# Reordering the last blocks of a single-core attention-and-MLP kernel, with a tail by priority, a held filler and one layernorm tile on ScalarE

## The chip, the cores and the metric

The kernel runs on one core of one Trainium2 chip. The metric is the device time of one execution in microseconds (us); a kernel's time is the median of several executions. A ratio between two kernels is the mean time of one kernel's runs over that of the other's of the same rounds on the same chip, so it is not quite the ratio of the medians quoted here. A clock given with a run is the mean granted TensorE clock.

The engines are written as the profile has them: PE is TensorE (PEld its weight loads), ACT is ScalarE, DVE is VectorE, POOL is GpSimd, SP is SyncE.

## The reference, cut to what matters

The input x is 2048 tokens by 448, in bfloat16. Attention has 16 heads of 28.

```python
xn = layernorm(x)
q, k, v = split(xn @ wqkv)                            # 16 heads of 28
s  = softmax(q @ k.T * 28 ** -0.5) @ v @ wo           # attention
g  = silu(gelu(xn @ w1 + b1) @ w2 + b2)               # dense layers, 448 -> 1792 -> 448
out = x + s * g
```

## The kernel before

Attention is done in blocks. A block is one head group (4 heads) on one query chunk (512 queries); there are 4 x 4 = 16 blocks of 64 score tiles, each 128 keys by 512 queries, 1024 tiles in all. A small scheduler in Python runs when the kernel is built. It holds every piece of work as a task with an engine, a planned duration and a priority, simulates the five engines, and writes each engine's instructions in the order that comes out. A change of a threshold or a priority therefore moves instructions about, nothing else.

```python
NP = 21                       # buffers of 128x512 for exp'd scores (P)
THS    = (8.0, 4.0, 7.0, 8.0, 4.0, 7.0, 9.0, 6.0, 6.0, 8.0, 8.0, 8.0, 8.0, 8.0, 7.0, 3.0)   # one per block
SLACKS = (6.0, 5.0, 3.0, 5.0, 2.0, 6.5, 9.0, 6.5, 3.0, 4.0, 7.0, 6.0, 8.0, 6.0, 8.0, 3.0)
HAM_WIN, HAM_LOW, DUM = 3.4, 0.85, 0.17
...
g, c = b // C, b % C          # block b: head group g on query chunk c
```

**Scores and exps.** TensorE writes three score tiles into PSUM (`ring`), ScalarE takes the exponential of the three in one instruction (a unit), and TensorE multiplies them with the values into `acc`. ScalarE is the bound, so the last tile of some units goes to VectorE instead, which scales it (0.69 us) and works out the exponential as a polynomial in integer and float arithmetic (`p_exp2`, five more instructions):

```python
def pick_late(self, u):       # does VectorE take the last tile of unit u?
    ...
    left = (n - 1 - r) / 3.0 * 1.364 + SLACKS[m // 64]       # time to the end of the block, plus a slack
    ...
    bl = K.backlog()                                          # what VectorE has queued
    if not K.ys or bl > THS[m // 64] or bl + 4.8 > left or sub > LATE_SUB:
        return False

def p_exps(self):
    ...
    yield ("until", lambda: all(K.PPREV[m] is None or K.pv_done[K.PPREV[m]] for m in ms))   # P buffer free?
    yield _Task(ACT, fexp, ...)

def p_pv(self):               # value matmuls; the last ones of a block wait for all of its VectorE tiles
    ...
    yield ("until", lambda: K.exp_m >= ms[-1] and K.E_done >= first - 1 and (
        not end or len([x for x in K.late_ready if K.sub_of(x[0]) == b]) == K.late_left[b]))
    ...
    if end:
        K.spawn(K.p_epi(b) if b < NBLK - 1 else K.p_epi4(first - NBLK + 1), 0.5)
```

**The end of a block** normalizes it. GpSimd splits the reciprocals of the row sums in two bfloat16 parts, and TensorE spreads these over the partitions:

```python
def p_epi(self, b):
    yield _Task(DVE, ...tensor_copy(E, K.acc)...)                                  # eviction
    yield _Task(PE, ...)                                                           # row sums
    yield _Task(DVE, ...reciprocal(K.rc, bank[:, 0:16])..., 0.26, 0.0, 1)
    yield _Task(POOL, ...tensor_copy(K.rhi, K.rc)..., 0.2, 0.0, 1)
    yield _Task(POOL, ...tensor_tensor(K.rlo, K.rc, K.rhi, ALU.subtract)..., 0.22, 0.0, 1)
    yield _Task(PE, ...)                                                           # spread rhi, rlo
    yield _Task(DVE, ...tensor_tensor(dst, bank2, E, ALU.mult)..., 0.7, 0.0, 1)
```

**Output.** When a chunk's four head groups are done, each of its four output tiles takes an output matmul, a multiplication by the gate g (0.62 us) and an addition of x (0.39 us) on VectorE, and a store. The last block is cut in three parts, so that only the last output tile is left at the very end (`p_epi4`, `p_norm4`, `p_last`):

```python
def p_norm4(self, t):
    yield _Task(PE, ...matmul(bank[:, 0:128], K.selb, E)..., 0.1, 0.12, 3)
    yield _Task(DVE, ...reciprocal(R, bank[:, 0:128])..., 0.96, 0.0, 1)
    yield _Task(DVE, ...tensor_tensor(dst, E, R, ALU.mult)..., 0.3, 0.0, 1)

def p_last(self, t):
    yield K.t_wo(ps, tok, c, t, (0, 1, 2), 3)
    yield ("until", lambda: K.on4[t])
    yield K.t_wo(ps, tok, c, t, (3,), 3)
    yield from K.t_oev(ps, tok, c, t)
```

**Filler.** A task of priority 95 adds empty matmuls when the planned TensorE activity of the last 3.4 us falls below 85%, to keep the granted clock up (`p_busy`, `pe_low`).

**Start.** x of chunk 0 is loaded in halves over two queues; VectorE does the layernorm statistics of all its tiles; x of chunk 1 is loaded after the first weights on SyncE's queue.

## Time and profile before

| | kernel before |
|---|---|
| time, median of 3 | 483.63 us (483.53 to 483.73) |
| the profiled execution by itself | 484.9 us, span 483.1 us, mean clock 0.993 |
| first exp begins | 13.14 us |
| first exp's start to last exp's end | 463.32 us |
| last exp's end to the end of VectorE | 4.46 us |
| VectorE's end to the end of the span (last store) | 2.15 us |
| tiles that VectorE takes | 76 of 1024 |

The four rows from the first exp to the last store are read from the trace and add up to the span. They are the frame.

How many tiles VectorE takes is read from the groups of instructions, as the count of the instruction that evicts a score tile to VectorE (line, engine, operation, tiles, count; busy us, mean ns; idle before it and its releaser):

```profile
L1183 DVE TENSOR_SCALAR x_sb<-ring 128x512 int32<-128x512 f32 x68 | 46.8, 688 | 14.2 <-PE ring L1129 13.0
L1274 DVE TENSOR_SCALAR x_sb<-misc 128x512 int32<-128x512 f32 x8 | 5.5, 686 | 1.8 <-PE misc L1270 1.8
```

That is 68 + 8 = 76 tiles; ScalarE has the other 948.

### The profile page before, as it was taken

The numbers are of one execution on the slowest core, as the hardware profiler recorded it, in microseconds if no ns is written. First come the engines' busy times: TensorE is split into PE (matmuls) and PEld (weight loads), VectorE is DVE, ScalarE is ACT, GpSimd is POOL, SyncE is SP. The second block draws the span as 40 slices with busy tenths as digits, with TensorE's granted clock in tenths as the row PEclk, the third lists the DMA queues.
The fourth block names the chain that finished last, engine by engine and source line by source line (L and its number), as shares of the span: only waits on it lengthen the run. The fifth ranks groups of instructions, "written<-read, shape, count | busy, mean of one in ns | idle before, by whom it ended". The sixth has DMA issues, their size and how long they took to land.

```text
span 483.1 us, 10155 instructions
## 1 busy us (share of the span) xinstructions
PE 438.5 (91%) x4232; PEld 168.1 (35%) x4268; DVE 407.6 (84%) x592; ACT 468.8 (97%) x390; POOL 43.2 (9%) x77
## 2 busy tenths in 40 slices
PE   6999899998889898999989988999999999999995
PEld 5442333332223333332323343333333333333453
DVE  8946888989978989989878749899997999889785
ACT  5999999999999999999999999999999999999994
POOL 7470000000010000000101000010100100100001
PEclk9998999999999999999999999999999999999998
DMA  8501000000000000000400000000101010011011
GB/s 247 149 9 28 1 0 2 1 2 2 0 1 1 1 1 1 1 2 1 134 1 0 1 2 0 1 2 1 38 1 40 1 38 1 23 37 58 3 39 39
DMA packets 8288, 11.08 MB, mean 23 GB/s; under 512 B 1650, under 2 KB 6898, under 8 KB 8243
## 3 DMA queue, kind: packets, MB, share of 16 engines
q1 hardware_dynamic: 8098, 10.21, 7.0%
q8 instruction: 33, 0.54, 0.5%
q10 hardware_dynamic: 144, 0.23, 0.1%
q14 instruction: 13, 0.10, 0.1%
HBM read 8.61 MB, written 1.84 MB: 22 GB/s over the span
## 4 chain that ended last, share of the span: by engine, by line
ACT 45%; PE 32%; issue 17%; DVE 5%; ACTq 0%; DVEq 0%
ACT P L1160 42%; PE ring L1129 9%; PE acc L1346 6%; PE misc L1065 4%; PE acc L857 3%; PE misc L695 2%; ACT h L1044 2%; PE misc L1007 1%; PE acc L839 1%; PE misc L949 1%; PE misc L1442 1%; PE ring L1007 1%; ACT w L1080 1%; PE ring L949 1%; DVE kT L1298 0%
## 5 line engine op out<-in xcount | busy, mean ns | idle before, releaser
L1160 ACT ACTIVATE P<-ring 128x1536 bf16<-128x1536 f32 (+1 forms) x350 | 428.9, 1469 | 1.7 <-PE ring L1129 1.5
L1129 PE MATMUL ring<-qT,kT 32*128 32x512 bf16 (+2 forms) x1144 | 136.5, 360 | 26.1 <-ACT P L1160 22.0
L1346 PE MATMUL acc<-P,vaug 128*32 128x512 bf16 (+2 forms) x1074 | 95.0, 363 | 1.0 <-issue 0.5
L1129 PEld LDWEIGHTS ring<-qT,kT 32*128 32x128 bf16 x1144 | 35.5, 91 | 132.8 <-ACT P L1160 123.5
L1183 DVE TENSOR_SCALAR x_sb<-ring 128x512 int32<-128x512 f32 x68 | 46.8, 688 | 14.2 <-PE ring L1129 13.0
L1065 PE MATMUL misc<-w,h 128*128 128x448 bf16 x224 | 52.3, 355 | 0.1
L1415 POOL CAST rhi<-rc 128x16 bf16<-128x16 f32 x15 | 10.3, 686 | 402.5 <-DVE rc L1413 255.6
L857 PE MATMUL acc<-ident,zero 128*128 128x128 bf16 x516 | 44.8, 221 | 0.0
L1346 PEld LDWEIGHTS acc<-P,vaug 128*32 128x32 bf16 x1074 | 24.4, 93 | 51.0 <-issue 46.6
L857 PEld LDWEIGHTS acc<-ident,zero 128*128 128x128 bf16 x516 | 29.8, 98 | 21.3 <-issue 19.4
L1007 PE MATMUL misc<-xnT,w 128*128 128x512 bf16 x127 | 35.9, 382 | 1.3 <-issue 0.8
L990 DVE CAST h<-misc 128x512 bf16<-128x512 f32 x35 | 24.1, 688 | 8.1 <-PE misc L1007 7.0
L1304 DVE SCALAR_TENSOR_TENSOR x_sb<-x_sb,kT 128x1024 uint16<-128x1024 int32 (+1 forms) x24 | 26.7, 1111 | 0.5
L1302 DVE SCALAR_TENSOR_TENSOR kT<-kT 128x1024 f32<-128x1024 f32 (+1 forms) x24 | 26.6, 1110 | 0.5
L1298 DVE SCALAR_TENSOR_TENSOR kT<-kT 128x1024 f32<-128x1024 f32 (+1 forms) x24 | 26.5, 1104 | 0.6
L1300 DVE SCALAR_TENSOR_TENSOR kT<-kT 128x1024 f32<-128x1024 f32 (+1 forms) x24 | 26.4, 1102 | 0.2
L1065 PEld LDWEIGHTS misc<-w,h 128*128 128x128 bf16 x224 | 17.3, 97 | 23.9 <-issue 12.1
L1007 PE MATMUL ring<-xnT,w 128*128 128x512 bf16 x82 | 19.3, 380 | 2.0 <-ACT h L1044 1.6
L1298 DVE SCALAR_TENSOR_TENSOR w<-w 128x1024 f32<-128x1024 f32 (+1 forms) x18 | 20.3, 1128 | 0.3
L1304 DVE SCALAR_TENSOR_TENSOR x_sb<-x_sb,w 128x1024 uint16<-128x1024 int32 (+1 forms) x18 | 20.3, 1130 | 0.2
L1300 DVE SCALAR_TENSOR_TENSOR w<-w 128x1024 f32<-128x1024 f32 (+1 forms) x18 | 20.3, 1130 | 0.2
L1302 DVE SCALAR_TENSOR_TENSOR w<-w 128x1024 f32<-128x1024 f32 (+1 forms) x18 | 20.3, 1129 | 0.1
(154 smaller groups left out, 449.6 us busy)
## 6 DMA issues: line engine op xcount, KB each, us to landing
h<-in_A_x_dram SPq DMA_DIRECT2D x4, 448.0 KB, 3.3
w<-in_B_w_dram SPq DMA_DIRECT2D x1, 1568.0 KB, 7.3
x_sb<-in_A_x_dram SPq DMA_DIRECT2D x3, 448.0 KB, 5.2
w<-in_B_w_dram SPq DMA_DIRECT2D x1, 1344.0 KB, 9.4
out_dram<-h SPq DMA_DIRECT2D x6, 224.0 KB, 1.9
h<-in_A_wqkv_dram SPq DMA_DIRECT2D x3, 168.0 KB, 5.5
out_dram<-h SPq DMA_DIRECT2D x4, 112.0 KB, 1.7
wo<-in_A_wo_dram SPq DMA_DIRECT2D x16, 24.5 KB
```

Of the source, the lines that this page charges most:

```text
L857: ins = eng.matmul(K.acc[:, 0:128], K.zero[:, :], K.ident[:, :], start=False, stop=True, skip_group_check=True)
L990: yield _Task(DVE, lambda eng: eng.tensor_copy(dst, bank), [tok], wr, 0.69, 0.0, 2)
L1007: ins = eng.matmul(bank, K.w1[:, kt, ft * 128:(ft + 1) * 128], K.xnT[:, kt, c * 512:(c + 1) * 512], start=(kt == 0), stop=(kt == KT - 1))
L1065: ins = eng.matmul(ps, hv[:, ft, t * 128:(t + 1) * 128], K.w2[:, ft, :], start=(ft == 0), stop=(ft == FT - 1))
L1129: return eng.matmul(K.ring[:, RB[m], col:col + nq], K.kT[32 * j:32 * j + 32, g, t * 128:(t + 1) * 128], K.qT[32 * j:32 * j + 32, g, c * 51 ...
L1160: return eng.activation(K.P[:, p0:p0 + n, :], K.ring[:, b0:b0 + n, :], ACTF.Exp, scale=SM_SCALE)
L1183: yield _Task(DVE, lambda eng, m=m, i=i, half=half: eng.tensor_scalar(K.ysb[i][:, 512 * half:512 * half + 512], K.ring[:, RB[m], :], SM_SC ...
L1298: yield _Task(DVE, lambda eng: eng.scalar_tensor_tensor(u, v, EXP_A, v, op0=ALU.add, op1=ALU.mult), [tv], [tu], d1, 0.0, 4)
L1300: yield _Task(DVE, lambda eng: eng.scalar_tensor_tensor(u, u, EXP_B, u, op0=ALU.add, op1=ALU.mult), [tu], [tu], d1, 0.0, 4)
L1302: yield _Task(DVE, lambda eng: eng.scalar_tensor_tensor(u, v, EXP_D, u, op0=ALU.mult, op1=ALU.add), [tv, tu], [tu], d1, 0.0, 4)
L1304: yield _Task(DVE, lambda eng: eng.scalar_tensor_tensor(pl.bitcast(dt.uint16), y, 2.0 ** -9, u, op0=ALU.mult, op1=ALU.add), ty + [tu], [K. ...
L1346: return eng.matmul(K.acc[32 * j:32 * j + 32, q0:q0 + nq], K.vaug[:, t, 4 * g + j, :], ap[:, col:col + nq], tile_position=(0, 32 * j), sta ...
```

## The change

Its intent: let both last blocks work on the last query chunk, so that the outputs of the other three chunks are out of the way of the last block; order the tail by priority, looking ahead for a more important task that is about to be ready; hold the filler matmuls back while the end of a block is on its way; move one small addition from GpSimd to VectorE; and shorten the start with ScalarE's sums and an earlier load of x. The thresholds of the offload were tuned again with it. The cuts leave out, among others, two planned durations in the last gate (the tanh 0.87 us for 0.47, the multiplication 1.03 for 0.85).

```diff
+GC = [(b // C, b % C) for b in range(11)] + [(3, 0), (3, 1), (3, 2), (2, 3), (3, 3)]
-THS = (8.0, 4.0, 7.0, 8.0, 4.0, 7.0, 9.0, 6.0, 6.0, 8.0, 8.0, 8.0, 8.0, 8.0, 7.0, 3.0)
-SLACKS = (6.0, 5.0, 3.0, 5.0, 2.0, 6.5, 9.0, 6.5, 3.0, 4.0, 7.0, 6.0, 8.0, 6.0, 8.0, 3.0)
+THS = (8.0, 4.0, 9.0, 8.0, 4.0, 7.0, 9.0, 6.0, 6.0, 8.0, 8.0, 4.0, 8.0, 4.0, 7.0, 5.0)
+SLACKS = (6.0, 8.0, 3.0, 5.0, 2.0, 6.5, 9.0, 6.5, 3.0, 4.0, 7.0, 6.0, 8.0, 6.0, 3.0, 3.0)
+TAIL = 18
 ... # the scheduler
-            self.pe_hist.append((start, start + t.dur))
+            self.pe_hist.append((start, start + t.dur * t.w))        # w: 0.15 and 0.3 for two thin matmul groups
-                    if s is not None:
+                    if s is not None and not (self.hold and p[3].E == PE and p[3].prio >= 90):
+            if self.exp_m >= MTOT - TAIL and E in (PE, DVE):
+                for s2, p2 in sorted(((c[0], c[1]) for c in cand), key=lambda c: c[0]):
+                    if p2[3].E == E and p2[3].prio < p[3].prio and s2 < s + p[3].dur - 0.1:
+                        s, p = s2, p2
+                        break
 ... # the start: loads, and one layernorm tile of chunk 0 on ScalarE
+        K.dma(ACT, lambda eng: eng.dma_start(K.x_sb[:, 1, :, :], xr[1]), K.s_x[1], writes=[K.b_x[1]], land=6.5)
-        ld(K.x_sb[:, 1, :, :], xr[1], K.s_x[1], [K.b_x[1]], 8.0)
+    def p_sums(self, i):
+        yield _Task(ACT, lambda eng: eng.activation(junk, x, ACTF.Copy, accum_out=K.st6[:, i, 0:1]), ...)
+        yield _Task(DVE, lambda eng: eng.tensor_scalar(m, K.st6[:, i, 0:1], 1.0 / D, None, op0=ALU.mult), ...)
+        yield _Task(ACT, lambda eng: eng.activation(junk, x, ACTF.Square, bias=m, scale=-1.0, accum_out=K.st6[:, i, 1:2]), ...)
 ... # the end of the last gate
-            yield _Task(POOL, lambda eng: eng.tensor_tensor(o, o, fb[:, 3, :], ALU.add), ..., 0.85, 0.05, 0)
+            yield _Task(DVE, lambda eng: eng.tensor_tensor(o, o, fb[:, 3, :], ALU.add), ..., 0.4, 0.0, 0)
 ... # the block order, in the scores, the value matmuls and the outputs
-                    g, c = b // C, b % C
+                    g, c = GC[b]
 ... # the end of a block: filler held from the last value matmuls to the eviction
             if end:
+                K.hold = True
 ...
         K.E_done = b
+        K.hold = False
 ... # the tail: priorities 0 to 2 for the last tile; the output matmuls split by head group
-        yield K.t_wo(ps, tok, c, t, (0, 1, 2), 3)
+        for g in range(G - 1):
+            yield K.t_wo(ps, tok, c, t, (g,), 3)
-        yield K.t_wo(ps, tok, c, t, (3,), 3)
+        yield K.t_wo(ps, tok, c, t, (3,), 3 if t < 3 else 1)
```

## The prediction

> **What bounds the kernel now.** I read the page's busy shares first, then ScalarE's groups and its waits, then a table of stretches, and last the timelines of the two ends, where ScalarE isn't the whole story.
>
> The busy line and the costliest group of the page (line, engine, operation, tiles, count; busy us, mean ns; idle before it):
>
> ```profile
> PE 438.5 (91%) x4232; PEld 168.1 (35%) x4268; DVE 407.6 (84%) x592; ACT 468.8 (97%) x390; POOL 43.2 (9%) x77
> ...
> L1160 ACT ACTIVATE P<-ring 128x1536 bf16<-128x1536 f32 (+1 forms) x350 | 428.9, 1469 | 1.7 <-PE ring L1129 1.5
> ```
>
> ScalarE (ACT) is busy 97% of the span, nearly all in L1160, the exps of the attention scores, and it sat idle only 1.7 us before them. The table of stretches (length; then busy us of PE, PEld, DVE, ACT, POOL; granted TensorE clock, DMA share, GB/s) cuts the run at the first exp (13.14 us) and at the end of ScalarE's exp work (476.05 us):
>
> ```profile
> 13.14:476.05 462.91, 426.92 (x4140) 160.65 (x4174) 391.78 (x545) 461.15 (x373) 31.63 (x47) 1.00 0.05 16
> 44.00:46.00 2.00, 2.00 (x10) 0.35 (x9) 0.87 (x2) 1.85 (x2) 0.00 (x0) 0.50 0.00 0
> 46.00:48.00 2.00, 1.84 (x16) 0.68 (x13) 1.41 (x3) 1.16 (x1) 0.00 (x0) 0.85 0.00 0
> 476.05:483.10 7.05, 2.34 (x25) 0.92 (x25) 4.28 (x9) 0.87 (x2) 2.06 (x2) 0.79 0.15 49
> ```
>
> So the time is three terms: a start of 13.1 us, a middle of 462.9 us in which ScalarE is idle only 462.91 - 461.15 = 1.76 us, and a tail of 7.05 us. Most of the idle 1.76 us is one hole: at 44 to 46 us the granted clock falls to 0.50, and ScalarE is then short of scores. The timeline shows the hole (start us, us, engine, line, tiles, [idle before <- releaser]):
>
> ```profile
> 44.75 1.03 PE L695 MATMUL misc<-xnT,wq 128*128 128x512 bf16 x2
> ...
> 46.84 3.71 ACT L1160 ACTIVATE P<-ring 128x1536 bf16<-128x1536 f32 x3 [0.96 <-PE ring L1129]
> ```
>
> Two projection matmuls took 1.03 us where, at full clock, such a pair at 35.80 took 0.60; the scores queued behind them came late, and ScalarE stood for 0.96 us. The tail's timeline:
>
> ```profile
> 475.57 0.89 ACT L1160 ACTIVATE P<-ring 128x512 bf16<-128x512 f32 x1
> ...
> 476.70 0.41 PE L1346 MATMUL acc<-P,vaug 128*32 128x128 bf16 x16
> ...
> 477.16 0.29 DVE L1377 CAST E_sb<-acc 128x128 bf16<-128x128 f32 x1 [0.27 <-PE acc L1346]
> 477.44 0.63 DVE L1451 TENSOR_TENSOR h<-ring,h 128x448 bf16<-128x448 f32 x1
> ...
> 477.81 0.22 PE L1388 MATMUL ring<-E_sb,selb 128*128 128x128 bf16 x1
> 478.06 0.96 DVE L1391 RECIPROCAL w<-ring 128x128 f32<-128x128 f32 x1
> 478.11 1.03 POOL L1097 TENSOR_TENSOR h<-h,w 128x448 bf16<-128x448 bf16 x1
> ...
> 479.88 0.62 DVE L1451 TENSOR_TENSOR h<-ring,h 128x448 bf16<-128x448 f32 x1 [0.16 <-PE ring L1442]
> 480.54 0.39 DVE L1453 TENSOR_TENSOR h<-h 128x448 bf16<-128x448 bf16 x1
> ```
>
> This is a chain: last exp, value matmul (PV), eviction, row-sum broadcast, reciprocal, multiply, output matmul, gate, residual, store. The last VectorE (DVE) instruction ends at 480.93, so the store takes the last 2.2 us.
>
> **What the Trainium skill says.** "Perfetto Trace Analysis", section Identifying the Most-Contended Engine, takes occupancy as a fair measure of distance to the limit on ScalarE: the 97% agrees. "TensorE: Matmul & The Clock Gate", section What's actually happening, says the clock falls to half when a monitor finds TensorE idle over windows of about 3.4 us. The trace has the half clock (0.50), though the record there counts PE busy for all of the 2.00 us. "ScalarE: Activation LUTs", section What ACT_TABLE_LOAD costs, gives 186 ns + 0.833 ns per element for an ACTIVATE with immediate operands and 93 ns more for a pointer operand: for 448 elements 0.56 us, and 0.65 us with a bias pointer. The trace agrees: the 448-element copy at L714 takes 0.56 us. "GPSIMD Engine Reference", section 3.1, has a two-input add about twice as slow on GpSimd as on VectorE; here the 448-element pair is 1.03 against 0.39 us.
>
> **The change part by part.**
>
> *The start.* One of the first chunk's four layernorm tiles leaves VectorE: a statistics instruction of 0.61 us goes; a ScalarE Copy (est. 0.56 us, sum) and Square (est. 0.65 us, squares) come, with two tiny VectorE scalings (0.07 to 0.14 each, as colK's 0.14). ScalarE idles from 2.0 to 5.3 us, so room exists. But the chain is serial: Copy, scale, Square, scale, Ln. Both x halves are there by about 3.9 us; VectorE does two statistics to 4.95, an aggregate to 5.2, the third to 5.8; the mean's scaling is about as early as that third (a tie), so I put it at 5.85, Square 5.95 to 6.65, scaling, Ln at about 6.85 against 6.75 before. So the second half gains nothing directly. The gain is that the first half's two normalizations (0.37 each) run about 0.6 us earlier, off the second half's way (all four sat in 6.63 to 8.53). The second load of x, issued now from ScalarE's queue at about 1.2 rather than 3.40 (its landing took 5.2 us, to 8.6), lets chunk 1's statistics run earlier; before, those at 9.54 held back a critical copy that began at 10.13. Against it, 448 KB now share the DMA engines with the weights that ScalarE relays at 5.73. Net: 0.3 us earlier, anywhere from 0.3 later to 0.9 earlier.
>
> *The hole.* The scheduler's account of TensorE activity now counts the 12 one-column matmuls at 40.74 (0.44 us in all) at 0.15 of their planned time, and the epilogues' four-column ones at 0.3, so it adds filler where the clock fell. At 38 to 42 us these are just what the account overrated. I give it a 65% chance to fill the 0.96 us: 0.6 us.
>
> *Exps moved from ScalarE to VectorE.* A unit of three tiles follows the last by 1.33 us (chain of waits: 121.64, 122.97; 134.22 and 136.88 for two), one of two tiles by 14.88 / 16 = 0.93 us. So a tile taken away saves 0.40 us of ScalarE. On VectorE it costs 0.69 + 0.4 + 4 x 0.69 = 3.85 us alone, or about 3.3 in a pair (0.69 + (0.68 + 4 x 1.13) / 2). Now 68 + 8 = 76 tiles go there. The block order puts chunk 2's last head group at block 14 and the three others one block earlier. So the four output tiles of chunk 2, at 0.62 + 0.39 = 1.01 us, leave the last block (8 gates and only 2 moved exps there now): 4.0 us of VectorE come free where its idle time was 0.6 us, enough for one more tile, perhaps two; the threshold for that block goes from 3 to 5. But block 12 takes chunk 0's output work with 1.3 us idle, thresholds of blocks 11 and 13 go from 8 to 4, and VectorE's total work is the same. Filler held back at block ends frees part of the 4.1 us in which evictions waited for filler. Net: 1 to 2 tiles more, 1.5 x 0.40 = 0.6 us.
>
> *The tail.* PV waits for the last exp (ends 476.46) and then behind output matmuls until 476.70; split by head group and ordered by priority, it can go at about 476.55: 0.15 us. The broadcast matmul at 477.81 stood behind four output matmuls, one slot of 0.19 us. In all 0.35 us, if VectorE's other gate (477.44 to 478.07) also stays out of the reciprocal's way. The gate's add (1.03 us on GpSimd, ends 479.14) wasn't what ended the wait: the last gate started at 479.88 behind TensorE. Moved to VectorE (0.39 us) it should fit while TensorE does its last matmul; it gains nothing and could cost up to 0.3.
>
> **Sum:** 0.3 + 0.6 + 0.6 + 0.35 = 1.85 us, so 483.63 - 1.85 = 481.8; I say 481.7.
>
> **The rivals.** (1) *ScalarE stays the bound and little moves:* no tile more is offloaded, the hole moves elsewhere. For it: VectorE's total work is equal and it is 84% busy already; then only the ends count, 0.65 us, giving 483.0. (2) *TensorE's clock becomes the limit:* held filler and lighter accounting shift the activity, and half-clock stretches of a microsecond each open new holes. For it: one did so before; against: only one in 463 us, and held filler pauses below 1 us. It would be 484. (3) *The x load in front delays the weights,* ScalarE waits in order, and the first exp comes 0.5 later: 482.6 or so. (4) *Everything takes:* three tiles (1.2), hole (1.0), start 0.8, tail 0.6: 480.0.
>
> **Range and chances.** The four terms are about independent, each uncertain by 0.3 to 0.6 us, so about 1 us together; I take 480.1 to 483.2. A 2% change is 9.7 us, more than start, hole, tile and tail savings together could give; the added work is less still. Same 0.98.
>
> **What would show it.** First exp at about 12.8 us (start right) or past 13.1 (wrong). No clock below 0.9 and no ScalarE wait near 0.9 us before 50 us (hole). 77 or 78 scores evicted by VectorE at what are now L1183 and L1274, three or four of them in the last block (offload). From the last exp's end to the last VectorE instruction 4.1 us rather than 480.93 - 476.46 = 4.47, and the broadcast matmul directly behind its eviction (tail). The number is wrong if the middle gains a new wait of ScalarE for scores, or if the tile count moves by more than three.

## The result, and the profile after

The changed kernel took 484.13 us (median of 6, 484.01 to 484.83) against 483.68 us for the kernel before beside it (median of 6, 483.53 to 483.75). The ratio is 1.0013, with a 95% interval of 1.0 to 1.0026: the same within 2%, as expected, but on the slower side, and above the predicted range of 480.1 to 483.2 us.

The page's busy line and the exps' group of the changed kernel, and its two groups of tiles that go to VectorE:

```profile
PE 438.1 (91%) x4242; PEld 168.7 (35%) x4278; DVE 395.5 (82%) x570; ACT 471.4 (98%) x394; POOL 40.1 (8%) x76
...
L1191 ACT ACTIVATE P<-ring 128x1536 bf16<-128x1536 f32 (+1 forms) x350 | 429.8, 1496 | 0.7 <-PE ring L1160 0.5
...
L1214 DVE TENSOR_SCALAR x_sb<-ring 128x512 int32<-128x512 f32 x65 | 44.7, 688 | 16.0 <-PE ring L1160 15.1
L1305 DVE TENSOR_SCALAR x_sb<-misc 128x512 int32<-128x512 f32 x8 | 5.5, 685 | 1.8 <-PE misc L1301 1.8
```

VectorE's busy time fell from 407.6 to 395.5 us, and it takes 65 + 8 = 73 tiles, three fewer than before. ScalarE's idle time before the exps fell from 1.7 to 0.7 us, yet its work grew. The table of stretches of the changed kernel (columns as in the prediction; as there, the middle is cut a little before the last exp's end, which is at 476.45 us here and at 476.46 before, so that it is 0.4 to 0.6 us shorter than in the frame above):

```profile
13.12:475.85 462.73, 426.91 (x4155) 161.19 (x4188) 380.82 (x523) 461.97 (x373) 29.54 (x47) 1.00 0.05 16
44.00:46.00 2.00, 1.46 (x14) 0.41 (x12) 1.76 (x3) 2.00 (x3) 0.00 (x0) 1.00 0.00 0
475.85:482.60 6.75, 1.95 (x25) 0.66 (x22) 3.87 (x8) 1.05 (x3) 1.03 (x1) 0.85 0.10 34
```

The hole at 44 us is not there: the clock is 1.00 and ScalarE is busy for all of the 2.00 us. The middle has 462.73 - 461.97 = 0.76 us of ScalarE's idle time against 1.76 before. One microsecond less idle time and an equal middle (462.73 against 462.91): what the hole gave back, ScalarE's extra tiles took. (The hole will turn out to be an accident of the profiled execution of the kernel before.)

The timeline of the changed kernel's tail:

```profile
476.50 0.41 PE L1377 MATMUL acc<-P,vaug 128*32 128x128 bf16 x16
...
476.96 0.29 DVE L1409 CAST E_sb<-acc 128x128 bf16<-128x128 f32 x1
...
477.31 0.23 PE L1421 MATMUL ring<-E_sb,selb 128*128 128x128 bf16 x1
477.58 0.96 DVE L1424 RECIPROCAL w<-ring 128x128 f32<-128x128 f32 x1 [0.33 <-PE ring L1421]
...
478.85 0.38 DVE L1128 TENSOR_TENSOR h<-h,w 128x448 bf16<-128x448 bf16 x1
...
479.39 0.62 DVE L1486 TENSOR_TENSOR h<-ring,h 128x448 bf16<-128x448 f32 x1 [0.16 <-PE ring L1476]
480.05 0.39 DVE L1488 TENSOR_TENSOR h<-h 128x448 bf16<-128x448 bf16 x1
```

The last exp ends at 476.45. The value matmuls begin 0.05 us later (before: 0.24), the broadcast 0.86 us later (before: 1.35), and VectorE ends at 480.44, 4.0 us after the exp (before: 4.46). The addition that moved to VectorE (L1128) fits in front of the last gate, which waits for TensorE as before.

ScalarE's timeline at the start of the changed kernel:

```profile
4.17 0.58 ACT L656 ACTIVATE P<-x_sb 128x448 bf16<-128x448 bf16 x1 [2.15 <-DMA x_sb<-in_A_x_dram]
4.65 0.19 ACT L656 ACTIVATION_READ_ACCUMULATOR P<-x_sb 128x1 f32 x1
...
6.12 0.67 ACT L662 ACTIVATE P<-x_sb,mv 128x448 bf16<-128x448 bf16 x1
6.69 0.19 ACT L662 ACTIVATION_READ_ACCUMULATOR P<-x_sb,mv 128x1 f32 x1
```

Each sum brings an instruction of 0.19 us that I had not counted, to read the accumulator. The first exp begins at 13.12 us in this execution, hardly earlier than before.

### The profile page after: what moved, and what is told of

It is laid out like the page before. It is cut to its first block, busy times and chain, and to the rows that moved or that the text cites. A ratio compares the mean times of both kernels' runs of the same rounds, so it can differ in the third digit from the quotient of the medians.

```text
span 482.6 us, 10158 instructions
## 1 busy us (share of the span) xinstructions
PE 438.1 (91%) x4242; PEld 168.7 (35%) x4278; DVE 395.5 (82%) x570; ACT 471.4 (98%) x394; POOL 40.1 (8%) x76
## 4 chain that ended last, share of the span: by engine, by line
ACT 47%; PE 31%; issue 17%; DVE 4%; ACTq 0%; DVEq 0%
ACT P L1191 44%; PE ring L1160 9%; PE acc L1377 5%; PE misc L1096 5%; PE acc L888 3%; ACT h L1075 2%; PE misc L1038 1%; PE misc L726 1%; PE acc L870 1%; PE misc L980 1%; PE ring L1038 1%; ACT w L1111 1%; PE misc L1476 1%; PE ring L726 1%; PE ring L980 1%
## 5 line engine op out<-in xcount | busy, mean ns | idle before, releaser
L1191 ACT ACTIVATE P<-ring 128x1536 bf16<-128x1536 f32 (+1 forms) x350 | 429.8, 1496 | 0.7 <-PE ring L1160 0.5
L1214 DVE TENSOR_SCALAR x_sb<-ring 128x512 int32<-128x512 f32 x65 | 44.7, 688 | 16.0 <-PE ring L1160 15.1
L1329 DVE SCALAR_TENSOR_TENSOR kT<-kT 128x1024 f32<-128x1024 f32 x20 | 24.3, 1216 | 0.5
L1331 DVE SCALAR_TENSOR_TENSOR kT<-kT 128x1024 f32<-128x1024 f32 x20 | 24.3, 1217 | 0.3
L1333 DVE SCALAR_TENSOR_TENSOR kT<-kT 128x1024 f32<-128x1024 f32 x20 | 24.4, 1218 | 0.2
L1335 DVE SCALAR_TENSOR_TENSOR x_sb<-x_sb,kT 128x1024 uint16<-128x1024 int32 x20 | 24.3, 1215 | 0.2
L1335 DVE SCALAR_TENSOR_TENSOR x_sb<-x_sb,w 128x1024 uint16<-128x1024 int32 (+1 forms) x18 | 20.3, 1129 | 0.2
L1333 DVE SCALAR_TENSOR_TENSOR w<-w 128x1024 f32<-128x1024 f32 (+1 forms) x18 | 20.3, 1128 | 0.1
```

Of the source, the lines that this page charges most:

```text
L1191: return eng.activation(K.P[:, p0:p0 + n, :], K.ring[:, b0:b0 + n, :], ACTF.Exp, scale=SM_SCALE)
L1214: yield _Task(DVE, lambda eng, m=m, i=i, half=half: eng.tensor_scalar(K.ysb[i][:, 512 * half:512 * half + 512], K.ring[:, RB[m], :], SM_SC ...
L1329: yield _Task(DVE, lambda eng: eng.scalar_tensor_tensor(u, v, EXP_A, v, op0=ALU.add, op1=ALU.mult), [tv], [tu], d1, 0.0, 4)
L1331: yield _Task(DVE, lambda eng: eng.scalar_tensor_tensor(u, u, EXP_B, u, op0=ALU.add, op1=ALU.mult), [tu], [tu], d1, 0.0, 4)
L1333: yield _Task(DVE, lambda eng: eng.scalar_tensor_tensor(u, v, EXP_D, u, op0=ALU.mult, op1=ALU.add), [tv, tu], [tu], d1, 0.0, 4)
L1335: yield _Task(DVE, lambda eng: eng.scalar_tensor_tensor(pl.bitcast(dt.uint16), y, 2.0 ** -9, u, op0=ALU.mult, op1=ALU.add), ty + [tu], [K. ...
```

## The experiments

There were eighteen experiments, two of them (e1 and e16) the two kernels unchanged; all gave right results, and the kernel before ran beside each on the same chip. I had these questions. Is the hole at 44 us part of the usual execution? Which part of the change gains, and which loses? Are three tiles fewer on VectorE the loss, and why were they given up? The account of every profile, in the frame of the table above (us; two kernels are listed twice, by two profiles):

| kernel | tiles on VectorE | first exp | first to last exp | last exp to VectorE's end | median | ratio to before |
|---|---|---|---|---|---|---|
| before | 76 | 13.14 | 463.32 | 4.46 | 483.63 | |
| e1: before again | 76 | 13.24 | 462.11 | 4.46 | 483.86 | 0.9998 |
| changed, first profile | 73 | 13.12 | 463.33 | 4.00 | 484.13 | 1.0013 |
| e16: changed again | 73 | 12.76 | 463.34 | 3.99 | 484.24 | 1.0010 |
| e2: changed, old thresholds | 75 | 12.85 | 463.92 | 3.99 | 485.00 | 1.0019 |
| e3: thresholds alone | 73 | 13.24 | 463.75 | 4.33 | 485.55 | 1.0033 |
| e4: start alone | 76 | 12.96 | 462.12 | 4.46 | 483.74 | 1.0000 |
| e5: tail alone | 76 | 13.21 | 464.08 | 4.96 | 486.25 | 1.0054 |
| e6: order and thresholds | 73 | 13.24 | 463.34 | 4.33 | 485.00 | 1.0024 |
| e7: changed, other thresholds | 75 | 12.84 | 462.92 | 3.99 | 483.72 | 0.9998 |
| e8: changed, old order | 76 | 12.77 | 465.26 | 4.00 | 484.05 | 1.0011 |
| e9: changed, third tile in last block | 74 | 13.25 | 462.91 | 4.95 | 484.75 | 1.0020 |
| e10: e2 with 24 buffers | 75 | 12.74 | 462.52 | 3.99 | 483.31 | 0.9990 |
| e11: changed, 76 tiles, 24 buffers | 76 | 12.76 | 464.63 | 3.99 | 485.35 | 1.0029 |
| e12: start and account | 76 | 12.72 | 462.12 | 4.46 | 483.36 | 0.9993 |
| e13: e5 without the hold | 76 | 13.21 | 464.06 | 4.95 | 485.55 | 1.0028 |
| e14: e5 with the account | 76 | 13.20 | 462.65 | 4.96 | 486.19 | 1.0034 |
| e15: e12, 77 tiles, 24 buffers | 77 | 12.96 | 461.94 | 4.37 | 483.20 | 0.9983 |
| e17: e5, casts on VectorE | 76 | 13.21 | 462.07 | 4.95 | 484.22 | 1.0011 |
| e18: e11, casts on VectorE | 76 | 12.75 | 461.88 | 3.99 | 483.05 | 0.9982 |

A profile shows one execution. Where a kernel's executions fall in two groups, its profile belongs to one of them, and the text says to which. "Account" is the weight w on the planned TensorE activity.

### Is the hole usual? (e1_before_again, e16_change_again)

Nothing is edited: e1 is the kernel before, e16 the changed one.

> The kernel before, unchanged, to see what its usual execution looks like and how large the noise is. The times on record are 483.5 to 483.75 us, but the profiled execution took 484.9 with a span of 483.1, so a usual span would be near 481.9. Theory 1 (the hole at 44 to 48 us, clock 0.50, was an accident of that one execution): clock 0.997 or more, no ScalarE wait over 0.5 us before 50 us, span 481.8 to 482.2. Theory 2 (the hole is in every execution of the kernel before): span 482.9 to 483.3, clock about 0.993, the 0.96 us wait again. Ratio to before 1.000 within 0.001.

> The changed kernel, unchanged, for a second profile: the first was of an execution at 484.64 us, 0.5 above the median, with the first exp at 13.12 us, where other kernels with the same start have it at 12.72 to 12.85. Theory A (that execution's start was late by chance): first exp at 12.7 to 12.85, stretch from first to last exp 463.3 as in the first profile (1.2 more than the kernel before, three tiles at 0.40), last exp to last VectorE instruction 3.99, span 482.2. Theory B (the late start belongs to the changed kernel and the others gained elsewhere): first exp at 13.1 and a span of 482.6.

In e1's profile (483.75 us) the stretch that held the hole reads:

```profile
44.00:46.00 2.00, 1.84 (x18) 0.58 (x15) 1.52 (x3) 2.00 (x3) 0.00 (x0) 1.00 0.00 0
```

The clock is 1.00 and ScalarE busy for all of it; the middle is 462.11 us rather than 463.32. So the hole is not in the usual execution. Of the 52 executions of the kernel before that ran beside my experiments, 8 had a mean clock of 0.993 or 0.994 and took 485.1 to 485.3 us; the other 44 had 0.996 or more and took 483.6 to 484.4. The profile (484.9 us, 0.993) was of the rare kind. The eight were not profiled; if each of them had the hole, filling it is worth some 1.4 x 8 / 52 = 0.2 us of the mean time and nothing of a median.

With e16 against e1, usual against usual, the change reads: start 13.24 to 12.76 = -0.48, middle 462.11 to 463.34 = +1.23, tail 4.46 to 3.99 = -0.47; the spans are 482.0 and 482.2. The middle loses 1.23 us for three tiles, 0.41 us each, and it is all work: the page has ScalarE idle for 0.7 us before the exps in both kernels, and busy with them for 428.6 us in e1 and 429.8 us in e16 (as in the changed kernel's first profile, shown above). That is the tile's price in the prediction (0.40), with the other sign. e1's group of exps:

```profile
L1160 ACT ACTIVATE P<-ring 128x1536 bf16<-128x1536 f32 (+1 forms) x350 | 428.6, 1466 | 0.7 <-PE ring L1129 0.5
```

### The thresholds (e2_old_thresholds, e3_thresholds_alone, e7_change_75_tiles)

e2 is the changed kernel with the kernel before's `THS` and `SLACKS`, e3 the kernel before with the new ones (the four lines of the change's diff, backwards and forwards); e7 is the changed kernel with others that give 75 tiles. e7's edit:

```diff
-THS = (8.0, 4.0, 9.0, 8.0, 4.0, 7.0, 9.0, 6.0, 6.0, 8.0, 8.0, 4.0, 8.0, 4.0, 7.0, 5.0)
-SLACKS = (6.0, 8.0, 3.0, 5.0, 2.0, 6.5, 9.0, 6.5, 3.0, 4.0, 7.0, 6.0, 8.0, 6.0, 3.0, 3.0)
+THS = (8.0, 4.0, 12.0, 6.0, 4.0, 7.0, 9.0, 6.0, 6.0, 8.0, 8.0, 7.0, 8.0, 4.0, 8.0, 5.0)
+SLACKS = (6.0, 8.0, 3.0, 5.0, 2.0, 7.5, 9.0, 6.5, 3.0, 4.0, 7.0, 6.0, 8.0, 6.0, 6.0, 3.0)
```

> The changed kernel with the old offload thresholds: 75 score tiles on VectorE instead of 73 (before: 76), everything else of the change kept. Theory A (ScalarE bounds, each tile that comes back to it costs 0.40 us): 484.13 - 0.8 = 483.3. Theory B (the new thresholds remove stalls at block ends, so the two tiles are paid for by waits of ScalarE for P buffers): 484.1 or more, with ScalarE waits over 0.5 us in the middle.

> The kernel before with the new thresholds alone: 73 tiles on VectorE instead of 76. Theory A: 3 x 0.40 = 1.2 us slower, 484.9, ScalarE busy 1.2 us more, DVE 10 to 11 us less. Theory B (VectorE's fewer tiles free it for evictions, the loss is made up): 483.7, same within 0.3.

> The changed kernel with thresholds that let 75 tiles go to VectorE where it has 73 (one more in blocks 11 and 14), placed so that no block waits for them. Theory A (the only thing lost is the tiles, 0.40 us each): 484.13 - 0.8 = 483.3, ScalarE's waits before exps 0.7 us as in the changed kernel. Theory B (any tile more in these blocks ends in a wait of ScalarE for a P buffer, as the 1.3 us with the old thresholds): 484.3 or more.

e3 shows the price of the new thresholds without anything else: 485.55 us, a ratio of 1.0033 (1.0020 to 1.0046). Its middle is 1.64 us longer than e1's; three tiles make 1.23 of it, and TensorE has a wait of 0.9 us for GpSimd in it that e1 has not (its kind comes up again below).

e2 shows that the old ones do not fit the new order as it stands. It gives two tiles back to VectorE and is slower still, 485.00 us (1.0006 to 1.0031 times before). Its timeline around the end of block 14:

```profile
451.45 0.62 DVE L1486 TENSOR_TENSOR h<-misc,h 128x448 bf16<-128x448 f32 x1 [0.40 <-PE misc L1476]
...
452.42 0.68 DVE L1333 SCALAR_TENSOR_TENSOR kT<-kT 128x512 f32<-128x512 f32 x1
...
453.14 0.69 DVE L1335 SCALAR_TENSOR_TENSOR x_sb<-x_sb,kT 128x512 uint16<-128x512 int32 x1
...
454.41 0.60 PE L1377 MATMUL acc<-x_sb,vaug 128*32 128x512 bf16 x5
...
455.11 2.79 ACT L1191 ACTIVATE P<-ring 128x1536 bf16<-128x1536 f32 x2 [1.31 <-PE acc L1377]
```

The output gates of chunk 2 (L1486; between the evictions that end blocks 13 and 14 lie ten gates, in the kernel before six) interleave with the polynomial of a late tile (L1333, L1335), which so ends only at 453.83. The block's last value matmuls have to wait for it, and while they wait no P buffer comes free: ScalarE stands 1.31 us at 455.11. The new order had moved the outputs of chunk 2 into block 14. Counted in the traces, the changed kernel has one tile fewer in each of the blocks 11, 13 and 14 (four for five) and two in the last block, as before. A tile fewer in block 14 fits this stop; why the tuning gave up those of blocks 11 and 13 no run shows.

e7 has five tiles again in blocks 11 and 14, without such a stop (no wait of ScalarE before an exp reaches 0.3 us in its trace). Its middle is 462.92 us, a gain of half of what two tiles are worth, and it ties with the kernel before. So at least these two tiles did not have to be given up.

### Are the P buffers the reason? (e10_old_thresholds_24_buffers)

e2 with three buffers more, so the wait's cause is taken away and not the wait:

```diff
-NP = 21
+NP = 24
```

> The changed kernel with the old thresholds (e2, 75 tiles, 485.0), with 24 buffers for exps instead of 21 and nothing else. Theory A (the stop of ScalarE at 452 us, 1.3 us of recorded wait and 1.85 us of lost spacing, is for a buffer that the value matmuls free late, because they wait at the block's end for a VectorE tile): the stop goes, 483.2 to 483.7. Theory B (it is the late tile itself, whatever the buffers): 484.8 to 485.1.

The stop is gone, the middle is 462.52 us (1.40 less than e2, and 0.41 more than e1 for the one tile fewer), and the median falls from 485.00 to 483.31 us (0.9976 to 1.0003 times before). The buffers were the reason for this stop. The changed order with the old thresholds wants 24 of them.

### Can the freed time in the last block be used? (e9_third_tile)

The prediction's case for the offload was that the last block loses output work. It did: from the end of block 14's eviction to the last exp's end VectorE is idle for 5.06 us in e1 and for 11.34 us in the changed kernel. e9 forces a third tile in:

```diff
-THS = (... 7.0, 5.0)          # of the last block
-SLACKS = (... 3.0, 3.0)
+THS = (... 7.0, 7.0)
+SLACKS = (... 3.0, 6.0)
```

> The changed kernel with the last block's thresholds raised (7 for 5, slack 6 for 3) so that a third tile goes to VectorE there (74 in all), into the 10 us in which VectorE is idle in that block. Theory A (as I predicted: the time freed there takes one more tile, worth 0.40 us): 483.7. Theory B (only the first half of the last block can use VectorE tiles, and a third one is late for its end): no gain, 484.2 to 484.8, a new wait of ScalarE or a longer stretch from the last exp to the last VectorE instruction.

The middle gains its 0.42 us, but the tail goes from 3.99 to 4.95 us: an output tile's gate and addition, 0.62 + 0.39 us, now come behind the last tile's chain instead of before it. The median is 484.75 us, slower than the change. With these priorities the freed time could not be turned into a tile's gain.

### The start (e4_start_alone, e12_start_and_account)

e4 is the kernel before with the start's part of the change as shown above (the load of x on ScalarE's queue, the sums on ScalarE); e12 has besides the weights w on the planned activity:

```diff
-        yield _Task(PE, f, K.b_wsq[g0:g1] + [K.b_pads], [tok], 0.15 * n + 0.1, 0.1, pr)
+        yield _Task(PE, f, K.b_wsq[g0:g1] + [K.b_pads], [tok], 0.15 * n + 0.1, 0.1, pr, 0.15)
-        yield _Task(PE, f, [tE, K.b_bsel], [tok], 0.25, 0.1, 3)
+        yield _Task(PE, f, [tE, K.b_bsel], [tok], 0.25, 0.1, 3, 0.3)
```

> The kernel before with the start alone: x chunk 1 from ScalarE's queue, one tile's layernorm sums on ScalarE; 76 tiles as before. Theory A (the chain Copy, scale, Square, scale, Ln takes as long as the statistics it replaces, the earlier first half gains nothing): first exp at 13.1, time 483.6 to 483.8. Theory B (the start does gain, and something later gives it back in the changed kernel): first exp before 12.9 and 483.4 or less.

> The kernel before with the start and the new account of TensorE activity (tiny matmuls count less, more filler), old order, tail and thresholds, 76 tiles. The start alone had two of five executions at clock 0.993 and 484.7. Theory A (the account keeps the clock): five of five at 0.996 or more, 483.4 to 483.7, no ScalarE wait over 0.5 us at 44 to 48 us. Theory B (it does nothing for it): one or two of five at 0.993 or below and 1.0 to 1.3 us longer.

The first exp begins at 12.96 (e4) and 12.72 us (e12); middle and tail are e1's to 0.01 us. Over all twelve profiles of kernels with this start the first exp begins at 12.87 us on average (12.72 to 13.25), over the eight without it at 13.21 us (13.14 to 13.24): 0.34 us gained, with a wide scatter from one execution to the next: two of the twelve, the changed kernel's first profile (13.12) and e9 (13.25), are as late as the eight. The way is the predicted one: from e1 to e16 the first half's normalizations begin at 5.99 instead of 6.83 us, and the copy that the prediction called critical at 9.51 instead of 10.24. e12's median is 483.36 us, 0.4 below the kernel before, though its interval (0.9981 to 1.0006) includes 1. Two of e4's five executions had a clock of 0.993 or 0.994 and took a microsecond more; none of e12's five did, and none of the 43 executions of the changed kernel (e16 included), e2, e7, e9, e10, e12 and e15, which all have the account, was under 0.996. That fits the account preventing the hole. But the 11 of e6 and e17, which lack the account, had none under 0.996 either, and e8, e11, e14 and e18, which have it, did have such executions. The falls in the profiles of e8 and e11 lie elsewhere (below); their other low executions, and those of e14 and e18, were not profiled. So it isn't settled.

### The order with the thresholds (e6_order_thresholds), and the change without the order (e8_old_order_76_tiles)

e6 is the kernel before with `GC` and the new thresholds alone. e8 is the changed kernel with the old order and thresholds tuned to it:

```diff
-GC = [(b // C, b % C) for b in range(11)] + [(3, 0), (3, 1), (3, 2), (2, 3), (3, 3)]
+GC = [(b // C, b % C) for b in range(NBLK)]
-THS = (8.0, 4.0, 9.0, 8.0, 4.0, 7.0, 9.0, 6.0, 6.0, 8.0, 8.0, 4.0, 8.0, 4.0, 7.0, 5.0)
-SLACKS = (6.0, 8.0, 3.0, 5.0, 2.0, 6.5, 9.0, 6.5, 3.0, 4.0, 7.0, 6.0, 8.0, 6.0, 3.0, 3.0)
+THS = (8.0, 4.0, 7.0, 8.0, 4.0, 7.0, 9.0, 6.0, 6.0, 5.0, 8.0, 8.0, 8.0, 8.0, 7.0, 4.0)
+SLACKS = (6.0, 5.0, 3.0, 5.0, 2.0, 6.5, 9.0, 6.5, 6.0, 4.0, 6.0, 5.0, 8.0, 6.0, 8.0, 3.0)
```

> The block order with the new thresholds, 73 tiles, without the start, the tail and the activity account; to set beside the thresholds alone (485.55 against 483.82). Theory A (the order moves VectorE work between blocks that is hidden anyway, two tiles in the last block in both): 485.3 to 485.7, the stretch from last exp to last VectorE instruction 4.3 to 4.5. Theory B (the order itself is worth more than 0.5, because the last block's emptier VectorE ends it earlier): 484.9 or less.

> Everything of the change but the block order, with thresholds that keep 76 tiles. Theory A (ends gain 0.1 to 0.3 at the start and 0.48 in the tail, the middle is that of before): 483.0 to 483.3, faster than both kernels. Theory B (without the order the tail's priorities push chunk 2's output work past the last exp): 483.8 or more, tail stretch over 4.4.

e6 reproduces the changed kernel's middle to 0.01 us (463.34) without the start and the tail; its median is 485.00 us. So the middle's loss belongs to order and thresholds. Its last store took 2.83 us in the profile against 2.15 elsewhere, which I did not look into.

e8's profiled execution is its slowest (486.06 us): the clock was at 0.50 from 428.3 to 435.1 us, and fell while TensorE stood 1.05 us for GpSimd, until 428.71. It shows one thing cleanly: the tail is 4.00 us with the old order too, so the tail's gain does not need the order. Its four undisturbed executions took 483.64 to 484.10 us, no faster than the kernel before, though start and tail should have given 0.8 us; none of these was profiled, and where that went stays open.

### The tail, and what it ran into (e5_tail_alone, e13_tail_without_hold, e14_tail_with_account, e17_tail_casts_on_vectore)

e5 is the kernel before with the tail's part of the change as shown above (the hold, the look-ahead, the priorities, the split output matmuls, the addition on VectorE) and 5.0 as the last block's threshold. e14 adds the account's two edits of e12; e13 takes the hold out:

```diff
             if end:
-                K.hold = True
```

> The kernel before with the tail's parts alone (priorities with look-ahead, held filler, split output matmuls, the gate's add on VectorE), old block order, old thresholds except that of the last block (5 for 3, so that 76 tiles stay on VectorE). Theory A (the tail's saving of 0.48 us from the last exp's end to the last VectorE instruction, 4.47 to 3.99, needs nothing else): that stretch 4.0, time 0.5 less than before, 483.2. Theory B (with chunk 2's output work still in the last block it is pushed behind, and the tail grows): the stretch 4.5 or more, 483.7 to 484.3.

> The tail alone in the old order (486.25, five of five at clock 0.991 to 0.996), with the filler no longer held back at block ends; nothing else. Theory A (holding the filler starves TensorE at the last block's start until its clock halves, and ScalarE waits 2.2 us for scores): clock 0.997, no wait over 0.5 us there, 484.2, that is the kernel before plus 0.5 for the longer tail stretch (4.95 against 4.46). Theory B (TensorE's queue stands 1.5 us behind matmuls that wait for GpSimd's casts, held filler or not): clock 0.993 again, 485.5 to 486.3.

> The tail alone in the old order, filler held as in the change, with the new account of TensorE activity added. Theory A (the account alone makes up for the held filler): clock 0.997, 484.2. Theory B (it adds filler elsewhere, not where the queue stands): clock 0.993, 485.5 to 486.3.

All three lost: 486.25, 485.55 and 486.19 us. Four of e5's five executions, three of e13's six and four of e14's six had a clock of 0.990 to 0.995; the others of e13 and e14 lay at 484.7 to 484.9. e5's fifth took 486.35 us at 0.996, so the mean clock does not tell the groups apart without fail. e5's timeline (its table of stretches is further down):

```profile
454.02 1.18 DVE L1325 SCALAR_TENSOR_TENSOR kT<-kT 128x1024 f32<-128x1024 f32 x1
454.17 1.08 POOL L1445 CAST rhi<-rc 128x16 bf16<-128x16 f32 x1 [29.06 <-DVE rc L1443]
...
455.23 1.22 DVE L1327 SCALAR_TENSOR_TENSOR kT<-kT 128x1024 f32<-128x1024 f32 x1
455.33 1.20 POOL L1446 TENSOR_TENSOR rlo<-rc,rhi 128x16 bf16<-128x16 f32 x1
456.59 0.24 PE L1455 MATMUL misc<-ident,rhi 128*32 128x128 bf16 x4 [1.49 <-POOL rlo L1446]
```

The two small GpSimd instructions of 128x16 elements (a cast and a subtraction, called casts here) took 1.08 and 1.20 us. Each ended 0.05 to 0.08 us after a VectorE instruction with two inputs in SBUF (454.02 + 1.18, 455.23 + 1.22). Over all twenty profiles, the 302 such casts that began while VectorE was idle or read PSUM took 0.20 to 0.22 us each, and the 294 that began while it worked from SBUF to SBUF took 0.28 to 1.21 (208 of them beside an instruction with two inputs, 86 beside one with a single input); the scheduler plans with 0.20 and 0.22. The Trainium skill has this: "SBUF — State Buffer", section Who interferes with whom, says that a VectorE instruction with two SBUF inputs contends with a GpSimd instruction that reads SBUF, and that the later one is blocked until the first is done. The traces agree, with these numbers. TensorE's next matmuls in order were those that need the casts, so it stood 1.49 us, ScalarE ran short of scores by 0.57 us at 457.90, and the clock fell to half at 457.5.

I saw the pairing of casts and VectorE instructions only after e13 and e14, so e17 tests it: e5, with the casts of block 14's end on VectorE.

```diff
+        ce, cd = (DVE, 0.15) if b == NBLK - 2 else (POOL, 0.2)
-        yield _Task(POOL, lambda eng: eng.tensor_copy(K.rhi[:, :], K.rc[:, :]), [K.b_rc], [K.b_rhl], 0.2, 0.0, 1)
+        yield _Task(ce, lambda eng: eng.tensor_copy(K.rhi[:, :], K.rc[:, :]), [K.b_rc], [K.b_rhl], cd, 0.0, 1)
 ... # the subtraction in the same way
```

> The tail part alone (e5_tail_alone, 486.25 us), with the two small casts of block 14's epilogue moved from GpSimd to VectorE. In e5_tail_alone they took 1.08 and 1.20 us on GpSimd, each ending 0.05 us after a VectorE instruction with two SBUF inputs that ran at the time, against 0.20 and 0.22 where VectorE ran none; TensorE's queue stood 1.49 us behind them and the granted clock then fell to 0.50. Theory (GpSimd held off by VectorE stops TensorE's queue, and that idle time brings the clock down): no TensorE wait over 0.6 us between 452 and 460 us, no granted clock below 0.9 there in the profile, mean clock at 0.996 or over in at least four of five executions, and a median of 484.3 (484.0 to 484.9), near the fast executions of the same part, 484.7. Rival (the look-ahead and the priorities of the last units cost the time by themselves): the wait goes, but the median stays at 486 within 0.4 and the clock at 0.993.

The same place in e17's timeline:

```profile
454.13 0.17 DVE L1446 CAST rhi<-rc 128x16 bf16<-128x16 f32 x1
454.34 0.17 DVE L1447 TENSOR_TENSOR rlo<-rc,rhi 128x16 bf16<-128x16 f32 x1
...
454.57 0.24 PE L1456 MATMUL misc<-ident,rhi 128*32 128x128 bf16 x4 [0.28 <-DVE rlo L1447]
```

The wait is 0.28 us, no stretch of two microseconds up to 480 us has a clock under 0.95, all six executions have 0.996 or more, and the median is 484.22 us instead of 486.25: 2.0 us from two casts of sixteen columns. (One of the six took 485.56 us all the same, and was not profiled.) The middles of three profiles divide it: e17's is 462.07 us, e14's, with the wait (and the account) and no fall of the clock, 462.65, and e5's, with both, 464.08; so the wait itself costs 0.6 us and the fall 1.4. The rival, that look-ahead and priorities cost the 2.0 us by themselves, fell. What remains against the kernel before, 0.45 us, is the tail: 4.95 instead of 4.46 us, because one output tile's gate and addition came behind the last chain, as in e9.

That the wait brings the clock down follows from e5 and e17 together for this place, but not as a rule: e14's profiled execution (484.79 us) has the same 1.49 us wait without a fall, and so has e15 with one of 1.1 us elsewhere. The traces offer a reason. In all twenty, the clock changes only at multiples of 3.41 us from its first change, and that first change comes at 6.6 to 9.5 us, differently from execution to execution. The table of stretches, cut on this grid for e5 (first two lines) and for e14 (last two):

```profile
454.12:457.53 3.41, 1.79 (x59) 0.97 (x53) 2.56 (x3) 3.21 (x3) 2.28 (x2) 1.00 0.01 2
457.53:460.95 3.42, 3.42 (x30) 1.26 (x24) 2.79 (x3) 2.65 (x2) 0.00 (x0) 0.50 0.02 5
...
452.44:455.85 3.41, 2.51 (x47) 1.11 (x47) 3.34 (x6) 3.41 (x4) 1.61 (x2) 1.00 0.00 0
455.85:459.27 3.42, 2.69 (x67) 1.56 (x68) 2.57 (x4) 2.94 (x4) 0.67 (x1) 1.00 0.03 7
```

In e5 (and e13) the wait lies within one such stretch, which leaves TensorE busy for 1.79 of 3.41 us, and the clock falls at its end; in e14 the wait is split between two, and neither is as empty. That is argued from the traces and not tested, and it isn't a threshold: of the six falls between the first exp and the last, five follow a stretch in which TensorE was busy 0.47 to 0.69 of the time, but the hole of the kernel before follows one of 0.91 (it holds the twelve one-column matmuls), and three stretches of 0.59 to 0.68 (e3, and two in e15) were followed by none. The hold is not the cause of the wait, as e13 has it as well; whether it makes the fall more frequent (four of five against three of six) these counts don't settle.

### Versions that might beat both (e11_change_76_tiles_24_buffers, e15_start_77_tiles_24_buffers, e18_change_76_tiles_casts_on_vectore)

e11 is the changed kernel with 24 buffers and thresholds that give 76 tiles, e15 is e12 with 24 buffers and 77 tiles, e18 is e11 with e17's edit.

```diff
-NP = 21
+NP = 24
-THS = (8.0, 4.0, 9.0, 8.0, 4.0, 7.0, 9.0, 6.0, 6.0, 8.0, 8.0, 4.0, 8.0, 4.0, 7.0, 5.0)      # e11, from the change
-SLACKS = (6.0, 8.0, 3.0, 5.0, 2.0, 6.5, 9.0, 6.5, 3.0, 4.0, 7.0, 6.0, 8.0, 6.0, 3.0, 3.0)
+THS = (8.0, 4.0, 7.0, 8.0, 4.0, 7.0, 9.0, 6.0, 7.0, 8.0, 8.0, 7.0, 7.0, 8.0, 7.0, 3.0)
+SLACKS = (6.0, 5.0, 3.0, 5.0, 2.0, 6.5, 9.0, 6.5, 3.0, 1.0, 7.0, 7.0, 8.0, 6.0, 8.0, 3.0)
 # e15, from e12: NP as above, and
-THS = (8.0, 4.0, 7.0, 8.0, 4.0, 7.0, 9.0, 6.0, 6.0, 8.0, 8.0, 8.0, 8.0, 8.0, 7.0, 3.0)
-SLACKS = (6.0, 5.0, 3.0, 5.0, 2.0, 6.5, 9.0, 6.5, 3.0, 4.0, 7.0, 6.0, 8.0, 6.0, 8.0, 3.0)
+THS = (8.0, 4.0, 7.0, 8.0, 5.0, 8.0, 9.0, 6.0, 6.0, 8.0, 8.0, 8.0, 8.0, 7.0, 9.0, 3.0)
+SLACKS = (6.0, 5.0, 3.0, 5.0, 3.0, 7.5, 9.0, 6.5, 1.0, 2.0, 7.0, 8.0, 8.0, 6.0, 8.0, 3.0)
```

> The changed kernel with 24 buffers and thresholds that send 76 tiles to VectorE, as many as before. Theory A (the change lost only by its three tiles): 482.8 to 483.3, faster than both. Theory B (tiles in these blocks end in hidden waits, as the 75-tile version, which gained 0.41 instead of 0.8): 483.5 or more.

> The start and the account (483.36, old order, old tail), with 24 buffers and thresholds that send 77 tiles to VectorE, one more than before. Theory A (a tile is worth 0.40 us wherever it goes, if no buffer is missing): 482.9 to 483.1, the fastest of all. Theory B (VectorE has no time for it, the tile ends in waits at a block's end): 483.4 or more.

> The change with 24 P buffers and 76 tiles (e11_change_76_tiles_24_buffers, 485.35 us), with the same two casts moved to VectorE. Theory: the 1.80 us wait of TensorE at 457 us for GpSimd goes, and with it the half clock at 460; first to last exp falls from 464.63 to about 462.3 (462.1, as of the 76 tiles of the kernel before, to 462.9), and the median to 483.3 (482.9 to 484.2; the other fall of the clock, at 286 us, may stay in some executions). Rival (76 tiles with this block order run VectorE late however the casts are done): a wait of ScalarE for scores or buffers of about a microsecond appears elsewhere after 440 us and the median stays above 484.6.

e11 missed: 485.35 us, with a wait of TensorE for GpSimd of 1.80 us at 458.75 and half clock from 459.3 us on, and another fall of the clock at 285.2 us. e15 gave 483.20 us, 0.9983 of the kernel before (0.9969 to 0.9998). e18 took e11's wait away and with it the loss. Its exps' group, to be compared with the 0.7 us of idle time in the changed kernel:

```profile
L1191 ACT ACTIVATE P<-ring 128x1536 bf16<-128x1536 f32 (+1 forms) x350 | 428.5, 1484 | 0.5 <-PE ring L1160 0.3
```

Its middle is 461.88 us, its tail 3.99 and its median 483.05 us, 0.9982 of the kernel before (0.9970 to 0.9993). It has the lowest median and beats both kernels, by 0.2%; from e15 its interval does not separate it. Three of its six executions had a clock of 0.994 or 0.995 and took 483.4 to 483.8 us, the other three 482.5 to 482.7; the fall at 285.2 us that e11 showed may be behind that, but no profile of such an execution of e18 was taken.

## Why the prediction was wrong

**The step that failed is "Exps moved from ScalarE to VectorE", predicted as 1.5 tiles more and -0.6 us.** It was three tiles fewer and +1.23 us (e16 against e1), 1.8 us off. The price of a tile was right (0.40 predicted, 0.41 measured); the count had the wrong sign. Two inferences in it failed. The first: that output work taken out of the last block makes room for tiles there. VectorE's idle time in that block rose by 6.3 us, but the count stayed at two, and forcing a third (e9) gained 0.42 us in the middle and lost 0.96 us in the tail. And the prediction took VectorE's idle time there before the change for 0.6 us, where the traces have 5.06. The second: I named the thresholds of blocks 11 and 13 that went from 8 to 4, and set them aside because VectorE's total work was the same. They were where the tiles went: blocks 11 and 13 lost one each, and block 14 a third, whose slack fell from 8 to 3, which I had not named. Taken by itself, a lower threshold or slack admits fewer tiles to its block. For block 14 the runs show what can go wrong: the outputs of chunk 2 had moved there, and a late tile behind them holds up P buffers (e2: 1.31 us of ScalarE's time; e10: gone with 24 buffers). Why the tuning gave up all three is not shown; e7 has two of them back and gains. A slip beside this: the price of a tile in a pair on VectorE, 3.3 us, took 1.13 us from a mean over two sizes; the 1024-column instructions alone take 1.22, which gives 3.5.

**The hole (-0.6 us) was a mis-sized term.** It is absent from the changed kernel's profiles, as predicted, but from e1's as well, so that this doesn't show the change filling it. At most it was worth 0.2 us of the mean and nothing of a median, since only 8 of 52 executions of the kernel before have the clock and the time that go with it. The data said so: the profiled execution took 484.9 us with a clock of 0.993, and the median was 483.63. A profile must be held against the times before a wait in it is counted.

**The start (-0.3 us) was right**: 0.34 us on average, by the earlier first half and chunk 1. By the prediction's own sign the changed kernel's first profile (13.12 us, past 13.1) spoke against it and e16 (12.76) for it; one profile was too few to tell. In e16 Square begins at 5.95 us, as predicted, and the second half's Ln at 6.92 instead of 6.85; the readings of the accumulator (0.19 us each) were left out. In the first profile x arrived later, and they are at 6.12 and 7.10.

**The tail (-0.35 us) was right**: 4.46 to 3.99, that is 0.47 us, with the broadcast directly behind its eviction, the value matmuls 0.05 us behind the last exp, and the addition on VectorE fitting in without gain. e5, e9 and e17 show that the same priorities can also give 4.95 us, where one output tile slips behind the chain.

Corrected after the fact with these terms, the prediction's sum is 483.63 - 0.34 (start) + 0 (hole) + 1.23 (tiles) - 0.47 (tail) = 484.05 us, against the measured 484.13. **Of the rivals**, the first came nearest (the hole moves, only the ends count, 483.0): it lacked the lost tiles. The second (the clock becomes the limit, 484) met the time but not the mechanism: the changed kernel's profile has no fall of the clock. It did happen in e5, e8, e11 and e13.

## What to carry to other kernels

When a tuned offload comes with a change, read the direction of the retuned thresholds first and count the work they move; room freed in one block is worth nothing if the work put there makes the end later (e9). Hold the profile's own execution time against the median before you give a value to any wait in it. In a queue that runs in order, a tiny instruction on a slow engine can cost microseconds: here two 16-column casts on GpSimd, held off by VectorE, cost 2 us with the fall of the clock that followed (e5 against e17), and moving them made the slow e11 into the version with the lowest median.

## What the Trainium skill lacked or had wrong

- "ScalarE: Activation LUTs", section What ACT_TABLE_LOAD costs, has the time of an ACTIVATE but not that of its accumulator output: each one here brings a separate record, ACTIVATION_READ_ACCUMULATOR, of 0.19 us. The same section has back-to-back ACTIVATEs overlap by about 93 ns. That agrees roughly with the exps of three tiles that begin after idle time: they take 1.45 us (as at 457.90 in e5), and back to back they follow each other by 1.33. What it lacks is that the record of a back-to-back one is longer, 1.60 us on average in the kernel before: records overlap by 0.27 us, so that a shorter wait of ScalarE need not show as idle time.
- "TensorE: Matmul & The Clock Gate", section HAM oscillation — how this bites in real kernels, gives gaps of TensorE over about 3.4 us as what brings the half clock. Here a single wait of 1.49 us (e5) was followed by it, after a stretch of 3.41 us in which TensorE was busy for 1.79. No page says how busy TensorE must be in such a stretch, and these runs don't settle it (falls after 0.47 to 0.69 and one after 0.91, none after 0.59 and 0.68).
- "SBUF — State Buffer", section Who interferes with whom, is borne out: 1.08 and 1.20 us instead of 0.20 and 0.22 for GpSimd's casts. No page gives what such a block costs further on, in the queue that waits for it: 1.49 us of TensorE, and 2.0 us of the kernel's time (e5 against e17).
